# Reordering the parts of a fused attention and feed-forward kernel behind its 292nd part

## The chip, the cores and the metric

The kernel runs on one core of a Trainium2 chip. The metric is device microseconds (us) of one execution, measured on the chip; lower is better. The engines are named as in the profile: PE multiplies matrices, DVE is VectorE, ACT is ScalarE, POOL is GpSimd, and SP issues the transfers (its queue is written SPq). Each engine works through its own instructions in order and waits on semaphores for the others.

## What is computed

```python
# attention: batch 4, heads 8, seq 768, head_dim 64; chunks of 32 keys, the best 6 are kept
k_min, k_max = per chunk minimum and maximum of k
ub   = sum(max(q * k_min, q * k_max))            # an upper bound for each chunk
top  = the 6 chunks with the largest ub, causal by chunk
attn = softmax(scale * q @ k.T, kept chunks and causal only)
x    = (attn @ v) laid out as 3072 tokens x 512
# feed-forward: 512 -> 2048 -> 512
h = x @ w_in
g = h * clip(h + 3, 0, 6) / 6
out = g @ w_out
```

## The kernel before

The 32 heads are 16 pairs i = 0 to 15. From pair 4 on, two pairs form a "quad" n = 2 to 7 (pairs 2n and 2n+1). The 3072 tokens are 8 groups g of 384 tokens, and each group is 3 blocks of 128. A group needs one half of a batch from all 4 pairs of that batch, so groups 2b and 2b+1 come after pairs 4b to 4b+3.

The order of all work is written out by hand: `ORDER` is a string of 1207 parts, and a loop at the end of the kernel calls a small function for each part, in that order. A part is a name and its numbers; letters at its end say which PSUM bank it uses (a, b, c are double banks PBa, PBb, PBc; x, y are single banks PSx, PSy). Each engine receives its instructions in the order of the parts. The parts that matter here:

- `lk.n`, `lq.n` (line 251) load k and q of a quad into a third of STAGE, four transfers each; `kd`, `qd` (line 257, DVE) turn them, `mx`, `mn`, `kx` (DVE) reduce k to chunk bounds, `rp`, `kb`, `qb` (ACT) prepare operands.
- `ud.n` (line 364) is 128 small matmuls for the chunk bounds; `us tr tm se tb tx` (DVE) turn them into a mask, `mv` (line 411, POOL) gathers it, `ms` (line 418) writes it to a scratch tensor SCR in DRAM and `ml.i.u` (line 426) loads pieces of it, replicated, into mask tiles (MX, MY, and free parts of WS and STAGE). Quads 2 and 3 apply the mask by matmuls instead.
- `SQ.n.u` (line 577) makes the scores of both pairs of a quad for one of six units u, into two banks; `ex.i.u` (line 588, ACT) takes the exponential, `af` (line 595, POOL) cuts the diagonal, `mm.i.u` (line 432, DVE) applies the mask.
- `A.i` (12 matmuls) and `B.i.0`, `B.i.1` (15 each) multiply with the values (line 611). A needs units 0 and 1, B needs units 2 to 5. `na`, `nb` (lines 628 and 631, DVE) normalise into XB.
- `xt.g` (line 637) issues three DMA transposes from XB to XT on SP. `H.g.f` (line 655) is 8 matmuls from XT, `hu` (line 663, ACT) and `gt` (line 666, DVE) make the gate GT. `O.g.t.n` (line 691) is 4 of the 16 matmuls of one output block, `ot` (line 698, ACT) copies it out of PSUM and `st` (line 702, SP) stores it.
- The last block, `O.7.2.0`, is made in two column parts (lines 680 to 683: 384 and 128 columns), each with its own ACT copy and store. The parts `O.7.2.1` and on, `ot.7.2` and `st.7.2` do nothing.

A bank is reused when its reader is done: `H` frees its bank after `gt`, `SQ` after `ex`, `A` and `B` after `na` and `nb`, `O` after `ot`, `ud` after `us`.

Of the kernel before, what the change touches and what calls it, by code (L numbers as in the profile page):

```python
# [34 lines left out]
PB LK.0.1.1 PW PI F1.b F0.b PT F4.a PO AQ.0.0.0 PF F3.x F7.c F5.b PZ AK.0.0.1 F6.b PC PR Z.y.6 LK.0.1.0 EG.3  # L35
KT.0.1.b F2.y MN.0.1 AQ.1.0.1 AQ.0.0.1 LK.3.0.1 QT.0.0.x MX.0.1 EG.1 PA RN.0.0 LK.0.0.0 KT.0.0.a MX.0.0 LQ.0.1.0
LQ.0.1.1 QT.0.1.y LK.1.1.0 AQ.1.0.0 LK.2.0.1 LK.1.1.1 MN.0.0 LK.1.0.0 LQ.1.1.0 EG.0 LQ.1.1.1 AK.1.0.1 KB.0.1
QT.1.0.c RN.1.0 RP.0.0 UH.0.0.b UB.0.0 QB.0.0 KT.1.1.x TH.0.0.b MX.1.1 T8.0.0 SE.0.0 KB.0.0 RA.0.1 RP.0.1 UH.0.1.a
UB.0.1 QB.0.1 QB.1.0 LQ.3.0.0 MN.1.1 RP.1.0 QT.1.1.y LH.0.0.b MT.0.0 KT.1.0.c LK.2.0.0 RP.1.1 MX.1.0 MN.1.0 LK.2.1.0
QB.1.1 KB.1.1 LQ.3.0.1 EG.2 S.0.1.b LQ.2.0.1 S.0.0.a ex.0.1 RN.1.1 TH.0.1.x T8.0.1 LQ.2.0.0 LK.3.0.0 KB.1.0 ex.0.0  # L40
af.0.0 UH.1.0.b QT.3.0.y RP.3.0 QB.3.0 SE.0.1 LK.2.1.1 LQ.2.1.1 UB.1.0 UH.1.1.c UB.1.1 KT.2.0.a RN.3.0 QT.2.0.b
RP.2.0 LH.0.1.c MN.2.0 QB.2.0 KT.3.0.y KB.3.0 MT.0.1 LQ.2.1.0 MX.2.0 KT.2.1.x S.0.5.c KB.2.0 RN.2.0 UH.2.0.b
TH.1.0.a ex.0.5 KB.2.1 MX.3.0 S.0.3.c ex.0.3 MN.3.0 af.0.3 T8.1.0 SE.1.0 QT.2.1.y RP.2.1 QB.2.1 UB.2.0 MX.2.1
LH.1.0.b MN.2.1 RA.2.1 TH.2.0.a MT.1.0 T8.2.0 TH.1.1.x UH.3.0.c SE.2.0 T8.1.1 wl.0 bd wc.0 S.1.1.b LK.3.1.1 ex.1.1
af.1.1 LH.2.0.a MT.2.0 UB.3.0 LK.3.1.0 KT.3.1.y KB.3.1 SE.1.1 LV.1.0.1 LQ.3.1.1 S.1.0.a UH.2.1.b MN.3.1 LQ.3.1.0
ex.1.0 UB.2.1 QT.3.1.x RP.3.1 af.1.0 LH.1.1.c MX.3.1 MT.1.1 LV.2.0.1 S.2.1.b S.2.0.a RN.3.1 TH.3.0.y S.0.2.c T8.3.0
af.0.5 ex.2.1 UH.3.1.b SE.3.0 QB.3.1 ex.2.0 LH.3.0.y UB.3.1 TH.2.1.x LV.0.0.1 LV.0.0.0 VC.0.0 MT.3.0 af.2.1 LV.1.0.0
T8.2.1 SE.2.1 S.0.4.b S.1.5.a ex.0.2 ex.1.5 af.2.0 LV.2.0.0 VC.2.0 TH.3.1.y T8.3.1 S.1.3.c ex.0.4 LH.2.1.x af.0.1
MT.2.1 A.2.a na.2 VC.1.0 ex.1.3 A.0.x na.0 lk.2 S.3.0.b ex.3.0 af.3.0 SE.3.1 S.1.2.a ex.1.2 af.1.2 S.3.1.c A.1.y
ex.3.1 LH.3.1.x kd.2.1 af.3.1 na.1 mn.2.1 af.1.5 af.0.2 MT.3.1 S.2.5.b ex.2.5 wl.1 af.2.5 LV.0.1.0 S.1.4.a ex.1.4  # L50
S.2.3.c LV.0.1.1 VC.0.1 X.0.0.x kd.2.0 LV.1.1.1 S.3.3.b mx.2.1 af.1.3 mn.2.0 LV.1.1.0 ex.2.3 S.2.2.a ex.2.2 VC.1.1
B.0.0.y B.0.1.y xe.0.0 LV.3.0.1 S.3.5.c LV.3.0.0 VC.3.0 ex.3.3 S.3.2.a nb.0 lk.3 A.3.x na.3 ex.3.2 LV.2.1.0 B.1.0.b
B.1.1.b nb.1 ex.3.5 af.3.3 X.0.1.y xe.0.1 mx.2.0 kx.2 S.2.4.c ex.2.4 kd.3.0 LV.3.1.1 mn.3.0 S.3.4.b ex.3.4 H.0.1.a
hu.0.1 X.1.0.c kd.3.1 kb.2.0 wc.1 H.0.2.b af.3.5 af.2.2 xe.1.0 af.3.2 LV.2.1.1 VC.2.1 gt.0.1 af.2.3 hu.0.2 B.2.0.y
B.2.1.y nb.2 LV.3.1.0 VC.3.1 B.3.0.x B.3.1.x nb.3 wl.2 gt.0.2 kb.2.1 wc.2 H.0.0.c hu.0.0 gt.0.0 H.0.3.a X.1.1.x
xe.1.1 H.0.5.b hu.0.3 gt.0.3 mx.3.1 hu.0.5 H.1.3.c gt.0.5 hu.1.3 wl.3 H.0.4.a hu.0.4 mn.3.1 H.1.1.b gt.1.3 gt.0.4
hu.1.1 lq.2 qd.2.1 gt.1.1 H.1.2.c hu.1.2 wl.4 wc.3 rp.2.1 wl.5 lq.3 H.0.6.a qd.2.0 gt.1.2 hu.0.6 gt.0.6 mx.3.0
rp.2.0 wc.4 wc.5 H.1.5.b hu.1.5 gt.1.5 qb.2.0 ud.2.a.c us.2.0 us.2.1 kx.3 tr.2.0 H.1.6.b tm.2.0 se.2.0 tb.2.0
O.0.2.0.x O.0.2.1.x hu.1.6 gt.1.6 qd.3.0 mv.2.0 mv.2.1 O.0.0.0.y H.1.4.a qd.3.1 wl.6 lv.4 wc.6 qb.2.1 hu.1.4 rp.3.1
tr.2.1 gt.1.4 tm.2.1 se.2.1 tb.2.1 O.0.0.1.y rp.3.0 H.0.7.b ud.3.a.c mv.2.2 us.3.0 tr.3.0 us.3.1 mv.2.3 kb.3.0  # L60
kb.3.1 O.0.2.2.x hu.0.7 gt.0.7 qb.3.0 H.1.7.a hu.1.7 gt.1.7 SQ.2.3.b.c tr.3.1 O.0.0.2.y tm.3.1 se.3.1 ex.4.3 wl.7
wc.7 SQ.2.2.a.b ex.5.3 O.0.0.3.y tm.3.0 tb.3.1 ex.5.2 af.5.2 lv.5 vc.5 lk.4 ex.4.2 H.1.0.c se.3.0 tb.3.0 mv.3.1 vc.4
ot.0.0 SQ.2.0.b.a hu.1.0 lq.4 gt.1.0 O.0.2.3.x ex.5.0 ot.0.2 O.0.1.0.y ex.4.0 kd.4.1 SQ.2.5.a.c ex.4.5 af.4.5 ex.5.5
af.5.5 af.4.0 qb.3.1 O.0.1.1.y O.0.1.2.y SQ.2.1.c.a mv.3.3 kd.4.0 ex.5.1 mn.4.1 af.5.1 st.0.0 mn.4.0 O.0.1.3.y
SQ.2.4.b.a mx.4.1 ex.4.1 af.4.1 ot.0.1 qd.4.0 O.1.1.0.y O.1.1.1.y af.5.3 af.5.0 qd.4.1 ex.4.4 mx.4.0 kx.4 rp.4.0
rp.4.1 A.5.x na.5 mv.3.0 kb.4.1 ud.4.c.b us.4.0 tr.4.0 us.4.1 tr.4.1 kb.4.0 O.1.1.2.y lv.7 vc.7 mv.3.2 ex.5.4
SQ.3.0.c.a ex.6.0 lv.6 vc.6 ex.7.0 st.0.2 af.6.0 A.4.x na.4 af.7.0 O.1.1.3.y SQ.3.1.b.c ex.7.1 tm.4.0 se.4.0 tb.4.0
ex.6.1 af.7.1 ot.1.1 B.5.0.x lk.5 B.5.1.x SQ.3.5.c.a af.6.1 nb.5 A.7.b na.7 A.6.y O.1.0.0.x na.6 af.4.2 ex.7.5
ex.6.5 af.6.5 qb.4.0 af.4.3 SQ.3.4.a.b tx.4.0 kd.5.0 tm.4.1 mx.5.0 O.1.0.1.x B.4.0.y lq.5 se.4.1 ex.7.4 SQ.3.3.c.b
# [692 lines left out]
```

## Time and profile before

| What | Value |
|---|---|
| Runs of before | 270.97, 271.82, 272.12 us; median 271.82 us |
| Span of the profiled execution | 272.2 us, its own time |
| PE busy | 258.0 us (95%) |
| DVE busy | 210.0 us (77%) |
| ACT busy | 180.5 us (66%) |
| POOL busy | 108.1 us (40%) |
| Transfers of the SP queue | 74.4% of the span of 16 DMA engines |

The profile gives no time for that execution apart from its span, which lies 0.4 us above the median. Busy shares are averages over the whole span; what bounds a stretch has to be read from that stretch.

### The profile page before, as it was taken

To read this page: it belongs to the slowest core of one execution; us is meant where nothing else is said; L and a number is where in the kernel's file an instruction comes from. 1 tells how busy PE (TensorE), PEld (TensorE's weight loads), DVE (VectorE), ACT (ScalarE), POOL (GpSimd) and SP (SyncE) were. 2 spreads that over 40 slices of the span, in tenths; PEclk is the share of its full clock that TensorE was granted. 3 is DMA by queue.
4 is the path that set the end of the run, shared out by engine and by line. 5 is a ranking of instruction groups with operands and counts; after the bars stand their busy time and mean duration, and the time that the engine had idled before them with its cause. 6 is when DMAs were issued, how large, how long until landed. Compare 5 with 4: busy or idle time off the path is not lost.

```text
span 272.2 us, 8580 instructions
## 1 busy us (share of the span) xinstructions
PE 258.0 (95%) x3442; PEld 149.7 (55%) x3442; DVE 210.0 (77%) x506; ACT 180.5 (66%) x249; POOL 108.1 (40%) x243
## 2 busy tenths in 40 slices
...
GB/s 166 203 245 181 257 199 361 250 249 339 197 174 235 135 55 156 303 105 235 209 230 133 206 194 205 179 221 177 124 198 167 213 164 135 45 54 116 39 2 117
DMA packets 105784, 48.80 MB, mean 179 GB/s; under 512 B 87184, under 2 KB 97680, under 8 KB 105744
## 3 DMA queue, kind: packets, MB, share of 16 engines
q1 hardware_dynamic: 103344, 47.66, 74.4%
...
## 4 chain that ended last, share of the span: by engine, by line
PE 63%; DVE 17%; DMA 9%; issue 5%; ACT 3%; SPq 3%; POOL 0%; DVEq 0%; ACTq 0%; POOLq 0%
PE PSy L691 11%; PE PSx L691 8%; PE PBa L655 8%; PE PBc L655 7%; PE PBb L655 5%; DVE GT L666 4%; DMA VS<-in_v_dram 4%; PE PBb L691 3%; PE PSx L611 3%; DVE PT L432 3%; DVE KMA L480 2%; DMA STAGE<-in_q_dram 2%; PE PBa L364 2%; PE PSy L611 2%; PE PBb L577 2%
## 5 line engine op out<-in xcount | busy, mean ns | idle before, releaser
L655 PEld LDWEIGHTS <-WIN 128*128 128x128 bf16 x512 | 49.0, 98 | 37.4 <-issue 4.1
L595 POOL TENSOR_SCALAR_AFFINE_SELECT PT<-PT 128x256 bf16<-128x256 bf16 x78 | 33.0, 443 | 69.2 <-ACT PT L588 68.8
L691 PEld LDWEIGHTS <-GT 128*128 128x128 bf16 x368 | 33.0, 98 | 37.0 <-issue 2.5
L691 PE MATMUL PSy<-WOUT,GT 128*128 128x512 bf16 x176 | 43.8, 380 | 0.0
L691 PE MATMUL PSx<-WOUT,GT 128*128 128x512 bf16 x144 | 35.6, 380 | 0.0
L411 POOL COPY MQA<-MTM 32x144 bf16<-32x144 bf16 x96 | 29.8, 311 | 11.8 <-DVE MTM L397 5.0
L655 PE MATMUL PBc<-XT,WIN 128*128 128x384 bf16 x176 | 32.2, 326 | 1.2 <-DMA XT<-XB 1.1
L655 PE MATMUL PBa<-XT,WIN 128*128 128x384 bf16 x176 | 32.2, 326 | 0.1
L666 DVE SCALAR_TENSOR_TENSOR GT<-U,PBc 128x768 bf16<-128x768 bf16 x22 | 20.9, 950 | 13.4 <-ACT U L663 13.3
L663 ACT ACTIVATE U<-PBc 128x768 bf16<-128x768 f32 x22 | 17.8, 811 | 19.2 <-PE PBc L655 19.1
L588 ACT ACTIVATE PT<-PBa 128x1024 bf16<-128x1024 f32 (+2 forms) x28 | 26.8, 958 | 5.5 <-PE PBb L577 3.5
L655 PE MATMUL PBb<-XT,WIN 128*128 128x384 bf16 x160 | 29.3, 326 | 1.0 <-ACT PT L588 1.0
L666 DVE SCALAR_TENSOR_TENSOR GT<-U,PBa 128x768 bf16<-128x768 bf16 x22 | 20.9, 948 | 11.9 <-ACT U L663 11.7
L663 ACT ACTIVATE U<-PBa 128x768 bf16<-128x768 f32 x22 | 17.9, 812 | 14.4 <-PE PBa L655 11.2
L588 ACT ACTIVATE PT<-PBc 128x1024 bf16<-128x1024 f32 (+2 forms) x26 | 23.6, 906 | 5.0 <-PE PBa L582 1.6
L588 ACT ACTIVATE PT<-PBb 128x1024 bf16<-128x1024 f32 (+2 forms) x24 | 21.5, 895 | 5.0 <-PE PBb L577 2.3
L257 DVE STREAM_TRANSPOSE STAGE<-STAGE 128x768 f32<-128x768 f32 x24 | 22.7, 964 | 1.7 <-DMA STAGE<-in_q_dram 1.5
L611 PEld LDWEIGHTS <-PT 128*128 128x128 bf16 x546 | 19.2, 97 | 6.9 <-issue 2.3
L663 ACT ACTIVATE U<-PBb 128x768 bf16<-128x768 f32 x20 | 16.3, 814 | 9.7 <-PE PBb L655 6.1
L666 DVE SCALAR_TENSOR_TENSOR GT<-U,PBb 128x768 bf16<-128x768 bf16 x20 | 18.9, 946 | 4.2 <-ACT U L663 4.2
L342 DVE TENSOR_REDUCE KMA<-STAGE 128x24 f32<-128x768 f32 x24 | 22.1, 937 | 0.1
L577 PEld LDWEIGHTS <-KBA 32*128 32x128 bf16 x480 | 9.7, 92 | 16.1 <-issue 13.2
...
## 6 DMA issues: line engine op xcount, KB each, us to landing
...
```

Source lines behind the costliest of these rows:

```text
L257: nc.vector.transpose(out=T, in_=T)
L342: nc.vector.tensor_reduce(out=dst, in_=staged("k", n)[:, h], axis=AX.X, op=(A.max, A.min)[w])
L411: nc.gpsimd.tensor_copy(to[:, part], rows)
L432: nc.vector.tensor_tensor(out=T, in0=T, in1=mask_tile(i, u).rearrange("p (k e x) -> p e k x", e=2, x=64), op=A.min)
L577: nc.tensor.matmul(PSB[both[g // 2]][:, g % 2, at:at + w], lhsT=K[rows, x, j * P:(j + 1) * P], rhs=Q[rows, x, q0:q0 + w], start=(x == 0), ...
L588: nc.scalar.activation(pt(i, u)[:, :, 0:n], PSB[slot["S", i, u]][:, :, 0:n], ACT.Exp, scale=float(scale))
L595: nc.gpsimd.affine_select(out=T[:, :, lo:lo + P], in_=T[:, :, lo:lo + P], pattern=[[0, 2], [1, P]], compare_op=A.is_ge, fill=0.0, base=0, ...
L611: nc.tensor.matmul(O[:, e, t, :], lhsT=pt(i, u)[:, e, lo:lo + P], rhs=VB[i % 4][:, j, e, :], start=(j == 0), stop=(j == qb))
L655: nc.tensor.matmul(PSB[c][:, ff, 0:GRP], lhsT=WIN[:, kt, (2 * f + ff) * P:(2 * f + ff + 1) * P], rhs=XT[g % 3][:, kt, :], start=(kt == 0), ...
L663: nc.scalar.activation(slot["R", g, f][:], PSB[slot["H", g, f]][:, :, 0:GRP], ACT.Relu, bias=3.0)
L666: nc.vector.scalar_tensor_tensor(out=GT[g % 2][:, 2 * f:2 * f + 2, :], in0=slot["R", g, f][:], scalar=6.0, in1=PSB[slot["H", g, f]][:, :, ...
L691: nc.tensor.matmul(PSS[c], lhsT=GT[g % 2][:, f, t * P:(t + 1) * P], rhs=WOUT[:, f, :], start=(f == 0), stop=(f == FT - 1))
```

## The change

The first 292 parts stay as they are (the last of them are S.3.4.b and ex.3.4). The other 915 are put into another order, and many are given other banks. No part is added or taken out, and no function changes. The line numbers behind the table are 2 lower afterwards. Two lines of the table as the diff has them, around the transposes of group 6:

```diff
-O.4.1.3.x ot.4.1 B.15.0.b B.15.1.b nb.15 xt.6 H.6.1.c hu.6.1 ml.14.2 mm.14.4 H.6.0.b ml.14.5 af.14.2 mm.14.2 gt.6.1
+ml.15.3 O.5.2.3.x ot.5.2 mm.15.3 B.12.0.c ot.4.1 B.12.1.c ml.14.2 xt.6 af.15.5 mm.15.5 nb.13 af.14.5 H.6.1.a hu.6.1
```

On PE the parts stand at nearly the same depth as before. Counted in PE's own work behind part 292, ud.2, SQ.2.3, H.2.2, SQ.4.0, B.8.0, H.4.0 and the first H.7 do not move at all. Some value products do: A.9 now comes 4.8 us of PE work later, B.10.0 6.1 us, B.12 10.6 us later.

**SP, around the transposes of group 6** (XT <- XB). SCR_110 and SCR_111 are the masks of pairs 14 and 15; OT rows are stores of output. Before:

```order
L702 DMA out_dram<-OT_134 128x512
L426 DMA STAGE<-SCR_111 128x1x768
L426 DMA MX_113<-SCR_110 128x1x768
L426 DMA MX_113<-SCR_110 128x1x256
L426 DMA STAGE<-SCR_111 128x1x768
L426 DMA STAGE<-SCR_111 128x1x256
L702 DMA out_dram<-OT_133 128x512
L426 DMA MY_116<-SCR_111 128x1x768
L426 DMA MY_116<-SCR_111 128x1x256
L637 DMA_TRANSPOSE XT_123<-XB_122 128x4x128 x3
L426 DMA WS_85<-SCR_110 128x1x768
L426 DMA WS_85<-SCR_110 128x1x256
```

Now:

```order
L700 DMA out_dram<-OT_134 128x512
L424 DMA MY_116<-SCR_111 128x1x768
L424 DMA MY_116<-SCR_111 128x1x256
L700 DMA out_dram<-OT_133 128x512
L424 DMA STAGE<-SCR_111 128x1x768
L424 DMA STAGE<-SCR_111 128x1x256
L424 DMA WS_85<-SCR_110 128x1x768
L424 DMA WS_85<-SCR_110 128x1x256
L635 DMA_TRANSPOSE XT_123<-XB_122 128x4x128 x3
L424 DMA STAGE<-SCR_111 128x1x768
L424 DMA STAGE<-SCR_111 128x1x256
L700 DMA out_dram<-OT_132 128x512
```

The load of unit 2 of pair 15 (the second STAGE pair) moved behind the transposes, that of unit 2 of pair 14 (WS_85) in front of them; the load of MX_113 moved further up.

**SP, around the load of q for quad 6.** SCR_104 and SCR_105 are the masks of pairs 8 and 9, XT_123 the transposes of group 3. Before:

```order
L637 DMA_TRANSPOSE XT_123<-XB_122 128x4x128 x3
L426 DMA WS_85<-SCR_104 128x1x768
L426 DMA WS_85<-SCR_104 128x1x256
L426 DMA MY_115<-SCR_105 128x1x384
L426 DMA MY_115<-SCR_105 128x1x256
L426 DMA MX_114<-SCR_104 128x1x768
L251 DMA STAGE<-in_k_dram 32x24x64 x4
L702 DMA out_dram<-OT_134 128x512
L426 DMA MX_112<-SCR_104 128x1x384
L426 DMA MX_112<-SCR_104 128x1x256
L251 DMA STAGE<-in_q_dram 32x24x64 x4
```

Now:

```order
L635 DMA_TRANSPOSE XT_123<-XB_122 128x4x128 x3
L416 DMA SCR_104<-MQA 128x1x1152
L260 DMA VS_69<-in_v_dram 128x12x64
L424 DMA MY_116<-SCR_105 128x1x768
L424 DMA MY_116<-SCR_105 128x1x256
L424 DMA MX_114<-SCR_104 128x1x768
L249 DMA STAGE<-in_q_dram 32x24x64 x4
```

Between the transposes and the load of q there were seven mask pieces, a store and the load of k; now there are three mask pieces, a load of v and the mask write SCR_104, which stood three rows above the transposes before.

**SP, the end of the program.** Before:

```order
L702 DMA out_dram<-OT_134 128x512
L702 DMA out_dram<-OT_132 128x512
L702 DMA out_dram<-OT_133 128x512
L683 DMA out_dram<-OT_134 128x384
L683 DMA out_dram<-OT_134 128x128
```

Now:

```order
L681 DMA out_dram<-OT_134 128x384
L681 DMA out_dram<-OT_134 128x128
L700 DMA out_dram<-OT_132 128x512
L700 DMA out_dram<-OT_133 128x512
L700 DMA out_dram<-OT_134 128x512
```

The block that is stored in two parts is no longer the last one; the program ends with a whole block of 512 columns.

## Rows read from the trace of the kernel before

**Rows 1.** The page, part 1: busy us, share of the span, instructions.

```profile
PE 258.0 (95%) x3442; PEld 149.7 (55%) x3442; DVE 210.0 (77%) x506; ACT 180.5 (66%) x249; POOL 108.1 (40%) x243
```

**Rows 2.** Stretches: us, then PE, PEld, DVE, ACT, POOL busy, clock, DMA, GB/s.

```profile
50.00:60.00 10.00, 8.80 (x115) 5.38 (x115) 10.00 (x13) 7.43 (x10) 4.02 (x3) 1.00 1.05 288
140.00:150.00 10.00, 9.11 (x126) 5.29 (x126) 9.93 (x17) 8.29 (x13) 7.82 (x13) 1.00 0.48 151
232.00:260.00 28.00, 28.00 (x167) 15.04 (x164) 12.02 (x14) 11.02 (x16) 0.00 (x0) 1.00 0.23 61
```

**Rows 3.** Waits of PE: line waited for; us in total, times, longest.

```profile
PE PBa L364 <- DVE GT L666: 1.2, 1, 1.2
PE PBc L655 <- DMA XT<-XB: 1.1, 1, 1.1
PE PBb L655 <- ACT PT L588: 1.0, 1, 1.0
PE PBc L577 <- issue: 0.9, 1, 0.9
```

**Rows 4.** The chain that ended last, late stretch: start us, us, what.

```profile
231.55 0.91 PE PSx L611 x30
240.25 1.30 PE PBa L655 x8
241.55 0.86 PE PSy L691 x4
```

**Rows 5.** Timelines of PE, DVE and SP, 157 to 168 us.

```profile
157.09 0.61 PE L611 MATMUL PBc<-VB,WS 128*128 128x65 bf16 x12
158.03 0.56 DVE L631 TENSOR_TENSOR XB<-PBc,RINV 128x384 bf16<-128x384 f32 x1
159.04 0.52 SPq L426 DMA_DIRECT2D MX<-SCR  x1
159.66 4.81 SPq L637 DMA_TRANSPOSE XT<-XB  x3
167.04 1.46 PE L655 MATMUL PBb<-XT,WIN 128*128 128x384 bf16 x8 [1.03 <-ACT PT L588]
```

**Rows 6.** Timelines of PE, DVE and SP, 215 to 227 us.

```profile
215.14 0.53 PE L611 MATMUL PSx<-VB,WS 128*128 128x65 bf16 x12
215.94 0.56 DVE L631 TENSOR_TENSOR XB<-PSx,RINV 128x384 bf16<-128x384 f32 x1
215.72 1.24 SPq L426 DMA_DIRECT2D STAGE<-SCR  x2
217.64 1.18 SPq L426 DMA_DIRECT2D MY<-SCR  x2
218.91 3.84 SPq L637 DMA_TRANSPOSE XT<-XB  x3
226.19 1.46 PE L655 MATMUL PBc<-XT,WIN 128*128 128x384 bf16 x8 [1.14 <-DMA XT<-XB]
```

**Rows 7.** Timelines of SP, DVE and PE, 127 to 149 us.

```profile
127.06 2.48 SPq L251 DMA_DIRECT2D STAGE<-in_q_dram  x4
135.32 1.84 DVE L257 STREAM_TRANSPOSE STAGE<-STAGE 128x768 f32<-128x768 f32 x2 [1.54 <-DMA STAGE<-in_q_dram]
142.69 1.09 PE L611 MATMUL PSx<-VB,PT 128*128 128x65 bf16 x30 [0.29 <-DVE PT L432]
148.48 0.47 PE L611 MATMUL PSx<-VB,PT 128*128 128x65 bf16 x10 [0.60 <-DVE RINV L628]
```

**Rows 8.** ACT at the end; landing of stores at L683, then at L702.

```profile
265.37 0.60 ACT L698 ACTIVATE OT<-PBb 128x512 f32<-128x512 f32 x1 [0.27 <-PE PBb L691]
268.86 0.28 ACT L682 ACTIVATE OT<-PBa 128x128 f32<-128x128 f32 x1 [0.40 <-PE PBa L680]
DMA to landing us min/median/max: 1.9/1.9/2.0
DMA to landing us min/median/max: 2.0/2.9/5.3
```

More of the change, by code (lines that the diff above doesn't have):

```diff
@@ L34 @@
 ORDER = """
[L35 to L69, printed above, removed]
```

123 lines of the change are left out of this document (78 added, 45 removed).

## Prediction

> **What bounds the kernel now.** I read four views in this order: the busy shares, the stretches, the waits of PE, and the timelines around each long wait. The busy shares show PE at 258.0 of 272.2 us [rows 1]; the reader should see from them that this change has little room. Nothing in it takes work from PE, and the 14.2 us in which PE is idle include the start, the end and the part before the 292nd, which stays. Late in the run PE is full: 28.00 of 28 us from 232 to 260 [rows 2]. There each `H` costs 1.30 us, a quarter of an `O` 0.86 us and a pair of `B` 0.91 us, start to start [rows 4]. So the new order can only win back time in which PE stood still.
>
> The waits of PE name where that is, behind part 292 [rows 3]. One wait of 1.2 us for a gate (line 666) before `ud.2`; 1.1 us for the transposes before `H.6.1`; 1.0 us before `H.4.0`; 0.9 us with no releaser that the profile shows, in `SQ.2.3`. Two shorter ones, 0.29 and 0.60 us, stand at `B.8` and `A.9` [rows 7]. Together that is 5.1 us, 1.9% of the span, and the most that this reading can give back.
>
> The wait of 1.0 us before `H.4.0` is put down to an ACT instruction. I read it as a wait for the transposes, by two rows [rows 5, 6]: in both places the first `H` starts 7.3 to 7.4 us after the first transpose was issued (159.66 to 167.04, and 218.91 to 226.19). That is the time that a group needs from its first transpose to its first matmul.
>
> **The change part by part.** The amount of work is the same on every engine, so each term is a wait that goes or comes.
>
> *Transposes of group 6.* `A.15` ends at 215.7, its normalise at 215.94 + 0.56 = 216.5, but SP was still issuing mask loads and a store and reached the transposes at 218.91 [rows 6]: 2.4 us lost in SP's queue. In the new order mask loads are earlier in front of them or behind them; of what stands directly in front, the load of unit 2 of pair 14 needs only `mm.13.2`, which DVE has before `na.15`. PE now has less work between `A.15` and `H.6.1`: seven `O` quarters, two `B` pairs and one `SQ` instead of eight, two and one, so 0.9 us less. The chain needs about 0.8 us to the normalise's end plus 7.3 us, 8.1 us; PE has 7 x 0.86 + 2 x 0.91 + 0.55 = 8.4 us. The wait of 1.14 us should go: -1.0 us (bounds 0 and -1.14).
>
> *Transposes of group 4.* The normalise of `A.11` ended at 158.03 + 0.56 = 158.6 and the transposes went out at 159.66, behind a mask load at 159.04 [rows 5]. That load now stands earlier. But DVE gets a k reduction of 0.94 us in front of `na.10` and `na.11`, which may eat part of the 1.1 us: -0.7 us (bounds 0 and -1.03).
>
> *DVE behind the load of q for quad 6.* The load was issued from 127.06 on and DVE stood still for 1.54 us until 135.32, waiting for its last piece [rows 7]. Right after, DVE is busy 9.93 of 10 us from 140 to 150 [rows 2], so this delay goes through to `B.8` and `A.9`. The new SP order issues that load earlier, DVE has `mm.8.2` after fewer long instructions, and `A.9` stands 4.8 us of PE work later. Both waits should go: -0.9 us (bounds 0 and -0.9).
>
> *The gate before `ud.2`.* From 50 to 60 us DVE is busy 10.00 of 10 [rows 2], and `ud.2` waits for `gt.0.6` behind it. In the new order the same number of instructions stands in front of `gt.0.6`; only one copy of about 0.5 us moves in front of a gate that DVE has to wait for anyway. `H.1.5` takes the bank of `H.1.2` instead of `H.1.1`, so a part of the wait moves one place forward. I take -0.4 us (bounds 0 and -1.2).
>
> *The gap in `SQ.2.3`.* The row shows no releaser [rows 3], so nothing says that another order removes it. The parts in front of it are the same set, in another sequence. I leave it at 0 (bounds 0 and -0.9).
>
> The Trainium skill (Runtime: NRT & Kernel Launch, Instruction fetch mechanics) says that an engine's instructions are fetched in blocks of 256 through a DMA queue of their own, ahead of use. By that rule a gap from a late fetch would stay where the instruction count puts it, and the sum would be the same; no row here shows that it is one.
>
> *The end.* Before, the last ACT copy takes 0.28 us and its store lands in 2.0 us. Now the last copy is one of 512 columns, 0.60 us, and a whole block's store lands in 2.0 us at best [rows 8]. +0.3 us for the copy and 0.1 us for the larger store: +0.4 us (bounds 0.3 and 1.2, the median landing of 2.9 us).
>
> The Trainium skill (DMA: Bandwidth & Descriptors, Anatomy of one DMA) gives, for transfers issued by GpSimd, 2.0 us plus the bytes at 436 GB/s. By it a store of 256 KB instead of 64 KB would cost 0.45 us more, an estimate from that page, and the sum would be 0.4 us worse; the landing rows of late stores are closer together than that.
>
> *New waits.* Two hand-overs of banks got shorter: `SQ.3.0` takes a bank of `ud.4` after one `A` instead of one `O`, and `H.5.7` follows its bank's last user by one `H` and one `O`. A reordering of 915 parts makes more of these than I can follow. I take +0.4 us (bounds 0 and 1.5).
>
> Sum: -1.0 - 0.7 - 0.9 - 0.4 + 0.4 + 0.4 = **-2.2 us**. Made against the profiled execution it gives 272.2 - 2.2 = 270.0 us; that execution is 0.4 us above the median of the runs, 271.8, so for a median I say **269.6 us**.
>
> **The rivals.** A difference under 0.5%, 1.4 us, cannot be told from no change here.
>
> *The waits only move.* PE is at 95%, DVE at 99% in one stretch. Where DVE is the bound behind PE, an earlier load lets it start earlier but it still has the same 9.9 us of work, and PE meets it a few parts later. Then I keep only the two transpose waits, 1.7 us, and pay the end and new waits at 1.5: 271.8 - 1.7 + 0.4 + 1.0 = 271.5 us. For it: PE does the same work at the same depth. Against it: the two transpose waits come from SP's queue, and DVE's load of 210 us is an average with room on both sides of that stretch.
>
> *Slower: the transposes of groups 6 and 7 become too tight.* This is one mechanism at one place, the last 55 us. PE work between `A.15` and `H.6.1` falls from 9.3 to 8.4 us, and between `B.14` and the first `H.7` from 11.2 (four `H`, seven `O`) to 9.1 us (three and six), while the chain stays at 8.1 us with nothing ahead of it. It decides when SP reaches the transposes more than 0.3 us late for group 6 or 1.0 us late for group 7; from there each us costs PE one. If SP is as late as before, 2.4 us [rows 6], group 6 waits 2.1 us (1.0 more than before) and group 7 waits 1.4 us. With the end and the new waits at 1.5, and the middle giving 0.7 back: 271.8 + 1.0 + 1.4 + 0.4 + 1.5 - 0.7 = 275.4 us; half of that lateness gives about 273.5. For it: seventeen mask loads and four stores of 0.6 us each must go out between the last mask write and the first of these transposes. Against it: the masks of quad 7 get ready earlier, since its `ud` moved 0.9 us forward.
>
> *The gap in `SQ.2.3` goes as well*, and all bounds on the good side hold: 271.8 - 1.14 - 1.03 - 0.9 - 1.2 - 0.9 + 0.3 = 266.9 us.
>
> **How the numbers follow.** My forecast, a gain of 1.4 to 3.9 us, gets 0.56; the full gain 0.05; waits that only move 0.29; too tight 0.10. Range: the forecast's own bounds go from 267.9 to 270.4. To hold 8 in 10 it must take in the waits that only move, so up to 272.1, and a part of the full gain, so down to 267.4. Faster by over 0.5% (under 270.4): 0.61. Within 0.5%: 0.29. Slower: 0.10.
>
> **What would show it.** In the new profile the waits of PE should no longer have a line of 1 us for the transposes or before `H.4.0`; from the normalise of `A.15` to the first transpose should be under 0.5 us. DVE should have no wait for a load of q. `ud.2` should still wait, about 0.8 us. The end should have one ACT copy of 0.60 us. I am wrong if PE's waits sum to as much as before under other names, if a DVE stretch near 140 is full and PE waits at its `A` and `B` again, or if the first `H.6` and `H.7` wait over 1 us for XT.

## The result and the profile after

| | before | changed |
|---|---|---|
| Median | 271.68 us (4 runs, 270.97 to 272.12) | 274.99 us (4 runs, 273.73 to 275.51) |
| Ratio | | 1.0138, interval 1.0092 to 1.0184 |
| Span of the profiled execution | 272.2 us | 273.8 us |

The changed order is slower; I had forecast 269.6 us, a gain. Twelve more runs of the changed kernel beside 29 of the one before (e5 below) give a smaller loss, 1.25 us between the medians and a ratio of 1.0069 with an interval from 1.0031 to 1.0107: the first four drew a large one. The ratios leave out runs over 1.5% above the fastest of the same kernel, a varying share of the runs here; so medians of all runs stand beside them below.

The busy shares of the changed kernel, against [rows 1]:

```profile
PE 259.8 (95%) x3442; PEld 150.5 (55%) x3442; DVE 210.8 (77%) x506; ACT 180.0 (66%) x249; POOL 107.7 (39%) x243
```

The same work on every engine, as it must be. The same stretches as [rows 2] (us, then busy of PE, PEld, DVE, ACT, POOL, clock, DMA, GB/s), and one that was unremarkable before:

```profile
50.00:60.00 10.00, 8.98 (x56) 5.28 (x54) 9.45 (x12) 6.50 (x9) 3.45 (x3) 1.00 1.13 305
140.00:150.00 10.00, 10.00 (x121) 5.64 (x118) 8.48 (x14) 9.38 (x14) 7.36 (x16) 1.00 0.79 184
156.00:164.00 8.00, 6.26 (x163) 3.88 (x162) 5.11 (x18) 1.02 (x2) 0.00 (x0) 0.79 0.28 76
232.00:260.00 28.00, 28.00 (x183) 15.67 (x181) 14.80 (x18) 11.29 (x15) 0.00 (x0) 1.00 0.18 52
```

From 140 to 150 us PE is now full (9.11 of 10 before), as forecast. From 156 to 164 us it loses 1.7 us and runs on a lower clock; before it was full there. The waits of PE, against [rows 3]:

```profile
PE PSx L609 <- DVE WS L430: 1.7, 1, 1.7
PE PSx L642 <- DVE MTM L540: 1.6, 1, 1.6
PE PBc L653 <- DVE GT L664: 1.0, 1, 1.0
PE PSy L609 <- DVE XT L646: 0.9, 1, 0.9
```

None of the four long waits of before stands where it was. Four others stand in their place, in this order at `A.11`, `X.0.0`, `H.1.5` and `B.2.0`; the one at `H.1.5` is the old wait for a gate ahead of `ud.2`, one place further forward. The second (`X.0.0`, at 34.58 us) lies ahead of part 292, and SP's first load from behind part 292 goes out only at 36 us or later, so the change can't have made it. Before it was 0.4 us.

Where the loss of that trace is: PE, DVE and SP around `A.11` and `ud.6`, against [rows 5].

```profile
156.71 0.22 PE L609 MATMUL PSx<-VB,WS 128*128 128x65 bf16 x2
158.66 0.48 PE L609 MATMUL PSx<-VB,WS 128*128 128x65 bf16 x10 [1.74 <-DVE WS L430]
151.78 0.35 DVE L430 TENSOR_TENSOR PT<-PT,WS 128x384 bf16<-128x384 bf16 x1
158.25 0.36 DVE L430 TENSOR_TENSOR WS<-WS 128x384 bf16<-128x384 bf16 x1 [2.92 <-DMA WS<-SCR]
152.05 0.54 SPq L700 DMA_DIRECT2D out_dram<-OT  x1
152.68 0.52 SPq L424 DMA_DIRECT2D WS<-SCR  x1
153.31 0.52 SPq L700 DMA_DIRECT2D out_dram<-OT  x1
160.88 4.44 SPq L635 DMA_TRANSPOSE XT<-XB  x3
```

The masks of unit 1 of all pairs share one tile, so `mm.10.1` (151.78) must be done before the load `ml.11.1` (152.68) may start, and `mm.11.1` (158.25) waits for it: landed at 158.16, 5.5 us after its issue. Before, the same load went out at 152.75 and landed after 3.8 us. Two stores of 256 KB stand right around it now. `H.4.0` itself has no wait any more; the stall has moved ahead of it.

The transposes of group 6, against [rows 6]:

```profile
217.84 0.20 DVE L626 RECIPROCAL RINV<-PBa 128x6 f32<-128x6 f32 x1 [0.44 <-PE PBa L609]
218.07 0.56 DVE L629 TENSOR_TENSOR XB<-PBa,RINV 128x384 bf16<-128x384 f32 x1
218.66 3.84 SPq L635 DMA_TRANSPOSE XT<-XB  x3
226.10 1.46 PE L653 MATMUL PBa<-XT,WIN 128*128 128x384 bf16 x8
```

From the end of the normalise (218.63) to the first transpose is 0.03 us, against 2.4 us, and the wait of 1.14 us is gone. DVE no longer waits for a load of q near 135 us and `B.8` starts without a wait, against [rows 7]:

```profile
138.96 0.96 DVE L255 STREAM_TRANSPOSE STAGE<-STAGE 128x768 f32<-128x768 f32 x1
142.89 0.63 PE L609 MATMUL PSx<-VB,PT 128*128 128x65 bf16 x15
```

The end, against [rows 8]:

```profile
267.97 0.60 ACT L696 ACTIVATE OT<-PSy 128x512 f32<-128x512 f32 x1 [1.99 <-PE PSy L689]
269.75 0.60 ACT L696 ACTIVATE OT<-PBa 128x512 f32<-128x512 f32 x1 [1.18 <-PE PBa L689]
```

One copy of 0.60 us, and its store lands at 272.38 us, 2.0 us after its issue, as forecast.

### The profile page after: what moved, and what is told of

Read it like the earlier page. It is cut to its first block, busy times and chain, and to the rows that moved or that the text cites. A ratio compares the mean times of both kernels' runs of the same rounds, so it can differ in the third digit from the quotient of the medians.

```text
span 273.8 us, 8570 instructions
## 1 busy us (share of the span) xinstructions
PE 259.8 (95%) x3442; PEld 150.5 (55%) x3442; DVE 210.8 (77%) x506; ACT 180.0 (66%) x249; POOL 107.7 (39%) x243
## 4 chain that ended last, share of the span: by engine, by line
PE 71%; DVE 13%; DMA 7%; POOL 3%; ACT 2%; issue 2%; DVEq 0%; ACTq 0%; POOLq 0%
PE PSx L689 11%; PE PSy L689 11%; PE PBc L653 8%; PE PBa L653 7%; PE PBb L653 7%; DMA WS<-SCR 3%; DVE PT L430 3%; DVE GT L664 3%; PE PBa L689 3%; PE PBc L575 2%; PE PSy L609 2%; DVE KMA L478 2%; DMA VS<-in_v_dram 2%; PE PBa L362 2%; PE PSx L609 2%
## 5 line engine op out<-in xcount | busy, mean ns | idle before, releaser
L593 POOL TENSOR_SCALAR_AFFINE_SELECT PT<-PT 128x256 bf16<-128x256 bf16 x78 | 31.7, 430 | 62.8 <-ACT PT L586 62.0
L689 PE MATMUL PSy<-WOUT,GT 128*128 128x512 bf16 x160 | 40.7, 385 | 0.0
L689 PE MATMUL PSx<-WOUT,GT 128*128 128x512 bf16 x160 | 39.7, 380 | 0.0
L409 POOL COPY MQA<-MTM 32x144 bf16<-32x144 bf16 x96 | 31.1, 324 | 17.7 <-DVE MTM L395 8.7
L653 PE MATMUL PBc<-XT,WIN 128*128 128x384 bf16 x184 | 33.7, 326 | 1.3 <-DVE GT L664 1.0
L653 PE MATMUL PBa<-XT,WIN 128*128 128x384 bf16 x168 | 30.7, 326 | 0.0
L586 ACT ACTIVATE PT<-PBa 128x1024 bf16<-128x1024 f32 (+2 forms) x27 | 25.4, 941 | 7.6 <-PE PBa L575 4.4
L586 ACT ACTIVATE PT<-PBc 128x1024 bf16<-128x1024 f32 (+2 forms) x27 | 25.0, 927 | 2.8 <-PE PBa L580 1.4
L664 DVE SCALAR_TENSOR_TENSOR GT<-U,PBa 128x768 bf16<-128x768 bf16 x21 | 19.9, 949 | 8.0 <-ACT U L661 8.0
L664 DVE SCALAR_TENSOR_TENSOR GT<-U,PBc 128x768 bf16<-128x768 bf16 x23 | 21.8, 946 | 4.1 <-ACT U L661 4.0
```

The lines of the kernel that those rows point to most:

```text
L409: nc.gpsimd.tensor_copy(to[:, part], rows)
L586: nc.scalar.activation(pt(i, u)[:, :, 0:n], PSB[slot["S", i, u]][:, :, 0:n], ACT.Exp, scale=float(scale))
L593: nc.gpsimd.affine_select(out=T[:, :, lo:lo + P], in_=T[:, :, lo:lo + P], pattern=[[0, 2], [1, P]], compare_op=A.is_ge, fill=0.0, base=0, ...
L653: nc.tensor.matmul(PSB[c][:, ff, 0:GRP], lhsT=WIN[:, kt, (2 * f + ff) * P:(2 * f + ff + 1) * P], rhs=XT[g % 3][:, kt, :], start=(kt == 0), ...
L664: nc.vector.scalar_tensor_tensor(out=GT[g % 2][:, 2 * f:2 * f + 2, :], in0=slot["R", g, f][:], scalar=6.0, in1=PSB[slot["H", g, f]][:, :, ...
L689: nc.tensor.matmul(PSS[c], lhsT=GT[g % 2][:, f, t * P:(t + 1) * P], rhs=WOUT[:, f, :], start=(f == 0), stop=(f == FT - 1))
```

## The experiments

All moves below are of whole parts; nothing else differs. "Order of before from part 700 on" means: the first 700 parts of one order, and after them those still missing, in the sequence of the other. Each group of runs (e1 to e4, e5 to e8, e9 to e12, e13 to e16, e17 and e18) shares one chip and its own runs of the kernel before. Each kernel has twelve runs, e7 six.

| Run | Edit | Median of all | Of before | Difference | Ratio (interval) |
|---|---|---|---|---|---|
| e1 | before again | 272.32 | 272.41 | -0.1 | 1.0009 (0.9972 to 1.0046) |
| e2 | new, mask chain mended | 273.69 | 272.41 | +1.3 | 1.0052 (1.0014 to 1.0090) |
| e3 | new to part 700 only | 272.59 | 272.41 | +0.2 | 1.0051 (1.0012 to 1.0090) |
| e4 | new from part 700 only | 275.04 | 272.41 | +2.6 | 1.0062 (1.0014 to 1.0110) |
| e5 | new again | 274.28 | 273.03 | +1.25 | 1.0069 (1.0031 to 1.0107) |
| e6 | new, `ud.6` later | 274.68 | 273.03 | +1.65 | 1.0079 (1.0037 to 1.0120) |
| e7 | new from 700 to 890 only | 275.81 | 273.03 | +2.8 | 1.0118 (1.0068 to 1.0168) |
| e8 | new from 890 only | 273.70 | 273.03 | +0.7 | 1.0042 (1.0006 to 1.0078) |
| e9 | new to 890 only | 273.29 | 273.26 | 0.0 | 1.0037 (0.9997 to 1.0077) |
| e10 | new, masks behind `na.13` | 274.34 | 273.26 | +1.1 | 1.0027 (0.9983 to 1.0070) |
| e11 | e2 + e10 + old end | 272.42 | 273.26 | -0.8 | 0.9993 (0.9953 to 1.0032) |
| e12 | e2, old from 890 | 274.25 | 273.26 | +1.0 | 0.9999 (0.9951 to 1.0048) |
| e13 | new, old end | 272.82 | 272.54 | +0.3 | 1.0016 (0.9982 to 1.0050) |
| e14 | new, stores early | 274.10 | 272.54 | +1.6 | 1.0056 (1.0027 to 1.0085) |
| e15 | e11 + stores early | 272.83 | 272.54 | +0.3 | 1.0015 (0.9975 to 1.0055) |
| e16 | before, stores late | 273.55 | 272.54 | +1.0 | 1.0069 (1.0031 to 1.0106) |
| e17 | before, `xt.6` earlier | 271.97 | 271.57 | +0.4 | 1.0014 (0.9977 to 1.0052) |
| e18 | e17 + `lq.6` earlier | 270.85 | 271.57 | -0.7 | 0.9948 (0.9909 to 0.9986) |

Twelve runs of one kernel spread over 2.5 to 9 us, and two medians of a dozen runs can differ by about 1 us by that alone. Medians and ratios do not always agree either: e3, e8 and e9 lie 0.2, 0.7 and 0.0 us over the kernel before by the medians, and 0.5, 0.4 and 0.4% (1.4, 1.1 and 1.0 us) by the ratios. So beside the times I read every trace by stretches: each part of PE gets its median duration from the first trace of before, and for each trace I note when PE has done the same amount of work. The change of that lag over a stretch is what the stretch cost more or less than in the first trace of before:

| Stretch there (us) | e1 | new | e5 | e2 | e9 | e14 | e15 | e17 | e18 |
|---|---|---|---|---|---|---|---|---|---|
| to 39 (unchanged parts) | +1.64 | +0.93 | +1.78 | +0.72 | +1.10 | -0.09 | -0.23 | +0.72 | +1.15 |
| 39 to 72 (`B.2`, gates, `ud.2`) | -0.94 | +0.67 | +0.68 | +0.67 | +1.69 | +0.67 | +0.67 | -0.93 | -0.93 |
| 72 to 78 (`SQ.2.3`) | -0.60 | -0.93 | -0.30 | -0.84 | -0.11 | -0.58 | -0.84 | -0.72 | 0.00 |
| 139 to 150 (q load, `B.8`, `A.9`) | -0.66 | -0.97 | -0.80 | -0.97 | -0.97 | -0.80 | -0.80 | +0.44 | -0.67 |
| 150 to 160 (`A.11`) | +0.06 | +3.30 | +1.40 | -0.18 | -0.03 | +1.50 | +0.36 | +0.37 | -0.07 |
| 160 to 172 (`H.4.0`) | -1.09 | -1.09 | -1.09 | -1.09 | -1.09 | -1.09 | -1.10 | -0.04 | -0.48 |
| 203 to 223 (`A.13`) | 0.00 | +0.49 | +0.88 | +0.84 | 0.00 | +1.21 | -0.47 | 0.00 | 0.00 |
| 223 to 234 (`H.6.1`) | +0.38 | -1.29 | -1.30 | -1.29 | -1.30 | -1.30 | -1.20 | -1.02 | -1.30 |
| end | +0.04 | +0.77 | +0.77 | +0.78 | -0.45 | +0.37 | -0.01 | -0.05 | -0.49 |

**The base.**

> The kernel before, once more, for the base of the sum. If the time of a run lies 1.7 us above its span, as in all runs of the changed kernel, the profiled execution with its span of 272.15 us was one of about 273.9 us, and a new one of about 271.7 us has a span of about 270.0 us; the parts that came 1.3 us earlier in the changed kernel's unchanged prefix show how much of that is jitter ahead of part 292. If the base was right, the span is 271.5 to 272.2 us again and the 1.7 us belong to the changed kernel alone. Time 271.0 to 272.2 us either way.

Span 271.0 us, time 272.73 us: 1.7 us apart, as in every run here that has both, to 0.1 us. By that the first trace of before, span 272.15 us, belongs to an execution of 273.9 us, outside the three runs shown. The second trace has other waits of PE:

```profile
PE PSx L644 <- DVE MTM L542: 2.2, 1, 2.2
PE PBc L655 <- DMA XT<-XB: 1.5, 1, 1.5
PE PBa L364 <- DVE GT L666: 1.2, 1, 1.2
PE PBc L577 <- issue: 0.3, 1, 0.3
```

The wait of 1.0 us before `H.4.0` is not there at all, that in `SQ.2.3` is 0.3 instead of 0.9 us, and DVE waits 0.78 us for the load of q, not 1.54. Three of the five waits that I meant to win are partly an accident of one execution.

**Cutting the order in two, at parts 700 and 890.**

```diff
-parts 292 to 1206: the order of before
+parts 292 to 699: the new order
+the parts left over: the order of before
```

(e3; e4 is the reverse; e8 and e9 the same with 890; e7 has the new order from 700 to 890.)

> Parts 292 to 700 in the new order, the rest as before. 'Mask chain': the loss lies behind part 700, so the time is that of before, 271.0 to 272.2, or up to 1 us less, since the wait for the load of q for quad 6 goes. 'Spread': about half of the loss, 273.0 to 273.8. 'Head': all of it, 274.5 or more.

> Parts 292 to 700 as before, the rest in the new order. 'Mask chain': all of the loss, 274.3 to 275.5, with a wait of over 1 us in A.11 for mm.11.1 in the trace. 'Spread': about half, 273.0 to 273.8. 'Head': as before, 271.0 to 272.2.

> Parts 700 to 890 in the new order (A.8 to H.4, some 137 to 180 us), all others as before. 'Mask chain': the whole loss of the kernel whose tail alone was new, so a median of 274.3 to 275.5 over all runs, half of them with a clock of 0.994 or less. 'Late' (the loss comes behind part 890, from the waits at 200 to 215 us and the end): 271.7 to 272.9.

> Parts 890 to the end in the new order, all before them as before. 'Mask chain': nothing of the loss, and the transposes of group 6 go out earlier, so 270.8 to 272.4. 'Late': 274.0 to 275.5. My forecast of +0.4 us for the end and -1.0 us for the transposes of group 6 would put it at 271.8 against 272.4 for the kernel before in that job.

> Parts 292 to 890 in the new order, the rest as before. In two jobs the changed order lay 1.3 us over the kernel before (medians of all runs), its head alone (to part 700) 0.2 us and its late part alone 0.7 us. 'Late' (new waits of about 1 us at A.13, where na.12 stands behind masks, and 0.35 us at the end): +0.2 to +0.7 us over the kernel before in this job, and no wait at A.13. 'Middle' (the wait in A.11 and what follows, parts 700 to 890): +1.0 to +1.6 us, with a wait for mm.11.1 in A.11 in the trace.

By the medians the head alone costs 0.2 us, the late part alone 0.7, head and middle together nothing; by the ratios they cost 0.5, 0.4 and 0.4%, with intervals that overlap. So the times rank no part above another. They do speak against "mask chain", which put all of the loss in the middle: the head and the late part, each without the new middle, have intervals above 1. e4 and e7, which were to show the middle, don't: where the old head meets the new middle, `SQ.5.0` waits for a gate, in e7

```profile
PE PBb L575 <- DVE GT L664: 3.1, 2, 2.9
```

a wait that neither whole order has. A cut is evidence only if its seam is clean in the trace.

**The mask chain and the two stores.**

```diff
 mm.9.3
+mm.10.1 ml.11.1
 ml.10.3
...
 na.8 st.2.0
-mm.10.1
 O.3.0.0.x
...
 hu.3.4
-ml.11.1
 vc.11
```

> The changed order, with mm.10.1 moved behind mm.9.3 on VectorE and the load ml.11.1 ahead of ml.10.3 on SP. Theory 'mask chain' (the loss is the late last link of the chain of masks of unit 1, which ends before A.11, and what follows from it): ml.11.1 goes out near 150.2 instead of 152.7, lands before 156, the wait of 1.7 us in A.11 goes, and the time falls by 1.2 to 2.5 us, to 272.5 to 273.8. Theory 'spread' (many small waits, each worth 0.2 to 0.5 us): the wait goes, but the time stays within 0.7 us of 275.0. Theory 'head' (lost ahead of part 700 and carried on): no change, 274.5 to 275.4.

> The changed kernel once more, for its spread over a dozen runs and a second trace. 'Mask chain': the chain of unit 1 ends so close to A.11 that the length of one load decides; so the runs spread, some near 272 us without the wait in A.11, most near 275; median of all runs 274.3 to 275.5, and the trace of a run under 273 has no wait over 0.5 us in A.11, that of a run over 274.5 has one. 'Spread': the traces of all runs have the same row of small waits, and the runs lie within 2 us of each other.

e2's trace has no wait in `A.11`, yet the median falls to +1.3 us only, and e5, with the order as it was, is at +1.25 us. e5's wait is shorter than in the first trace (its load landed after 5.0 us):

```profile
159.66 0.48 PE L609 MATMUL PSx<-VB,WS 128*128 128x65 bf16 x10 [1.25 <-DVE WS L430]
```

In the traces with the chain as the new order has it, `ml.11.1` takes 5.5, 5.0, 5.0, 4.2, 4.1, 3.5, 3.1 and 2.5 us (new, e5, e7, e10, e6, e4, e9, e13), and `A.11` waits 1.7, 1.3, 1.0, 0.5, 0.5, 0.2, 0 and 0 us: the longer this one load, the longer the wait. The old middle has the same load; it takes 3.6 to 4.3 us in seven traces, and the wait is 0 to 0.6 us. e12's trace shows what else stands in the way; its time says little, +1.0 us by the medians and no difference by the ratio.

```diff
 parts 292 to 889: as in the run with the mask chain mended
-parts 890 to 1206: the new order
+the parts left over: the order of before
```

> The changed order up to part 890 with the chain of masks of unit 1 mended, the rest as before. 'Middle': 0.5 us or more under the kernel with the late part old alone, so -0.3 to +0.4 us against the kernel before. 'Late': within 0.4 us of the kernel with the late part old alone. 'Head': both kernels stay at +0.7 us or more, since the mended chain gives nothing back to a head that is late.

```profile
160.18 0.60 ACT L696 ACTIVATE OT<-PSx 128x512 f32<-128x512 f32 x1 [2.01 <-DMA out_dram<-OT]
160.83 0.54 PE L609 MATMUL PSx<-VB,WS 128*128 128x65 bf16 x12 [1.31 <-ACT OT L696]
```

The mask is in time, but now the copy `ot.3.0` waits for `st.2.0`, issued at 155.13 and landed 4.9 us later, since the ring has three output buffers; `A.11` waits for the copy, since it takes its bank. e11 shows the same (1.97 and 1.27 us). At this place two transfers must be in time, and either was late in some trace. So I moved the stores:

```diff
 ml.10.1
+st.2.0 st.2.1
 SQ.5.4.c.b
...
 na.8
-st.2.0
 mm.10.1
...
 B.9.0.c
-st.2.1
 gt.3.4
```

> The changed order with the two stores st.2.0 and st.2.1 moved ahead in SP's queue, behind ml.10.1 (about 148 us instead of 152 and 153 us), nothing else. 'Stores' (at A.11 either ml.11.1 comes late beside the two stores, or the copy ot.3.0 waits for st.2.0 to land, by how long the transfers of that moment take): no wait over 0.6 us in A.11 by either way, median 0.4 to 1.0 us lower than the changed order, +0.3 to +0.9 us over the kernel before. 'Mask chain' (the load is late for its own reasons): the wait in A.11 stays, +1.0 to +1.6 us.

```profile
157.61 0.48 PE L609 MATMUL PSx<-VB,WS 128*128 128x65 bf16 x10 [1.36 <-DVE WS L430]
```

The stores now go out at 147.31 and 147.89 us, and the load still takes 4.7 us and `A.11` still waits: in this trace the load is late without the stores beside it. The opposite trial, stores late in the order of before:

```diff
-st.2.0
 mm.9.3
...
-st.2.1
 O.3.0.0.x
...
 O.3.2.1.y
+st.2.0
 ml.11.1
+st.2.1
 mm.11.1
```

> The kernel before, with st.2.0 moved directly ahead of ml.11.1 and st.2.1 directly behind it, as the new order has them; nothing else. 'Stores': +0.4 to +1.5 us over the kernel before, with a wait of A.11 for mm.11.1 or for ot.3.0 in the trace. 'Mask chain': ml.11.1 goes out 0.6 us later at most and nothing follows, -0.3 to +0.5 us.

+1.0 us, but not by the mechanism: its trace has no wait for `mm.11.1` or `ot.3.0`, and the mean granted clock was under 0.996 in ten of its twelve runs (in two to six of twelve in the others). In the traced one it was half from 21.2 to 28.1 us, ahead of everything that the edit moves. It says nothing for the stores; why the clock fell so often here, no run shows.

**`ud.6` right behind `A.11`.**

```diff
 na.11 ex.11.5 mm.10.3
-ud.6.a.c us.6.1 us.6.0 tr.6.0 tm.6.0
 O.3.2.1.y O.3.2.2.y
+ud.6.a.c us.6.1 us.6.0 tr.6.0 tm.6.0
 O.3.1.0.x
```

> The changed order, with ud.6 and the VectorE steps on it moved behind O.3.2.2, so that the small matmuls of ud.6 do not follow A.11's directly, as before. 'Mask chain': the wait in A.11 is as long as before the edit, so the median stays within 0.6 us of the changed kernel's in the same job. 'Clock' (the loss is the clock's fall to half in ud.6 and behind it): runs with a mean clock of 0.994 or less become rarer than one in five and the median falls by 0.8 to 1.7 us.

+1.65 us, no better; "clock" falls as a steady cause. In the first trace of the new order the clock did fall here: the stretch costs 3.3 us, 1.7 of them the wait, and the rest is about half of the 3.4 us that ran at half the clock (more below). But e5 has a wait of 1.25 us and the same sequence at full clock.

**`A.13`, and the end.**

```diff
 A.12.x ml.15.5
-mm.13.5
 SQ.7.5.b.c
-mm.13.3
 na.12
...
 na.13
+mm.13.5 mm.13.3
```

> The changed order with the masks mm.13.5 and mm.13.3 moved behind na.13 on VectorE, nothing else. B.13 alone needs them, 10 us of PE work later. 'Late': the waits of A.13 and SQ.7.4 (0.3 to 1.2 us together) go, and the median falls to +0.2 to +0.7 us over the kernel before. 'Middle': the waits go and the median stays at +1.0 to +1.6 us. A third way: the two masks turn up late at B.13 or hold up a load behind them, +1.3 us or more.

In e5 `A.13` waits for the normalise of `A.12`, which stands behind masks that no `A` needs; in e10 that wait is gone:

```profile
210.05 0.52 PE L609 MATMUL PSx<-VB,PT 128*128 128x65 bf16 x12 [0.82 <-DVE XB L629]
```

```profile
208.25 0.53 PE L609 MATMUL PSx<-VB,PT 128*128 128x65 bf16 x12
```

By the stretches it gives back 0.6 us (203 to 223 us: +0.78 on average over eight traces, +0.21 in e10), the median hardly moves (+1.1 against +1.25 us). The end alone:

```diff
 parts 292 to 1119: the new order
-parts 1120 to 1206: the new order
+the parts left over: the order of before
```

> The changed order with the parts from 1120 on as before (the last blocks' output, copies and stores), nothing else. 'End': 0.35 us for the last copy and its store, and whatever the new tail costs beside: +0.6 to +1.0 us over the kernel before in this job, where the changed order lay at +1.3 us. 'Waits' (the loss is the waits in the middle and at A.13): +1.0 to +1.6 us.

+0.3 us against +1.25: more was won than either theory said, and "end" (+0.6 to +1.0) is the nearer. Its trace shows 0.1 us less than the first trace of before behind the last matmul; the new end has 0.77 us more there, the same to 0.01 us in five of eight traces.

**All mended.** e11 has the chain, the masks and the old end; e15 the early stores too.

```diff
+mm.10.1, ml.11.1, mm.13.5, mm.13.3 as above; from part 1120 on the order of before
+e15 only: st.2.0 st.2.1 behind ml.10.1
```

> The changed order with three costs undone: the chain of masks of unit 1 (mm.10.1 behind mm.9.3, ml.11.1 ahead of ml.10.3), the masks of pair 13 behind na.13, and the end from part 1120 on as before. If the loss is the sum of these places, up to 0.5 us for the chain, 0.9 us for A.13, 0.35 us for the end, the gains that I forecast stand free: -0.7 to 0.0 us against the kernel before in this job. If the loss sits elsewhere (the head, which keeps a late start that the old order absorbs; SP's last drain, 0.45 us), +0.4 us or more.

> Stores early, chain of unit 1 mended, masks of pair 13 behind na.13, end as before, all else in the new order. If these four places are the loss, it is at or under the kernel without the first of them, which lay 0.8 us under the kernel before with an interval from -2.0 to +0.35 us: -1.5 to -0.5 us. If the rest of the new order costs as much as it wins, -0.3 to +0.5 us.

-0.8 and +0.3 us: level with before, and 1 to 2 us better against it than the whole new order (0.5 to 0.8% by the ratios). With these places mended the loss is gone, and nothing of the forecast gain shows either. e11's own trace still waits in `A.11`, so it is the two kernels together, more than one trace, that this rests on. e15's trace is the shortest of all, 268.6 us, with no wait in `A.11`, at `A.13`, at `H.4.0` or `H.6.1`. What it keeps is the head:

```profile
PE PBc L653 <- DVE GT L664: 1.0, 1, 1.0
PE PSy L609 <- DVE XT L646: 0.9, 1, 0.9
```

**The forecast gains alone, in the order of before.**

```diff
 mm.13.3
-ml.14.4
 B.13.0.b
...
 nb.15 xt.6
+ml.14.4
 H.6.1.c
```

> The kernel before, with one mask load of SP, ml.14.4, moved from ahead of the transposes of group 6 to behind them; nothing else. It makes the first of my terms alone: from na.15 to the first transpose under 1 us instead of 2.4, no wait of PE over 0.3 us for XT at the first H.6. If the term is what I forecast (-1.0 us, up to -1.5 by the second trace of the kernel before): -0.8 to -1.5 us. If another wait of that place takes over (B.15, B.14, the masks behind the transposes): -0.3 to +0.5 us.

```diff
 gt.3.3
+lq.6
 lk.7
...
 ex.8.3
-lq.6
 qd.6.0
```

> As the last one, and the load of q for quad 6 moved ahead of that of k for quad 7 on SP. It adds the term of VectorE behind that load (-0.9 us as forecast, -0.3 by the second trace of the kernel before). Both terms real: -1.5 to -2.4 us against the kernel before, no wait of VectorE for STAGE near 135 us. Absorbed (VectorE meets the same stretch of full work, or k of quad 7 is late instead): within 0.4 us of the run with the transposes alone.

In e17 SP reaches the transposes at 217.21 instead of 218.91 us and `H.6.1` has no wait, 1.0 us in the stretch; the median doesn't show it. In e18 they go out at 216.26 us and DVE has no wait for q:

```profile
216.26 3.85 SPq L635 DMA_TRANSPOSE XT<-XB  x3
133.96 1.83 DVE L255 STREAM_TRANSPOSE STAGE<-STAGE 128x768 f32<-128x768 f32 x2
```

By the ratio the two moves together are faster than before, 0.9948 with an interval from 0.9909 to 0.9986: the best of all kernels here. Being the best of many, and 0.7 us by the medians, it would need a second group of runs to be sure. The ratio makes it 1.4 us; both terms together were 1.9 us.

## Why the prediction was wrong

It said -2.2 us. Set against that, per stretch, the mean of all traces that have the old or the new order there (traces whose edit or seam lies in the stretch left out):

| Term | Stretch | Old order (traces) | New order (traces) | New less old | Forecast |
|---|---|---|---|---|---|
| Gate before `ud.2`, and `B.2.0` | 39 to 72 | -0.66 (8) | +0.92 (12) | +1.6 | -0.4, and in +0.4 |
| Gap in `SQ.2.3` | 72 to 78 | -0.46 (8) | -0.71 (12) | -0.25 | 0 |
| Load of q, quad 6 | 139 to 150 | -0.08 (5) | -0.88 (12) | -0.8 | -0.9 |
| `A.11` (a new wait) | 150 to 160 | +0.25 (6) | +1.03 (5) | +0.8 | in +0.4 |
| Transposes of group 4 | 160 to 172 | -0.58 (7) | -1.09 (10) | -0.5 | -0.7 |
| `A.13` (a new wait) | 203 to 223 | 0.00 (9) | +0.78 (8) | +0.8 | in +0.4 |
| Transposes of group 6 | 223 to 234 | -0.70 (7) | -1.25 (11) | -0.55 | -1.0 |
| End | behind the last matmul | -0.10 (12) | +0.62 (8) | +0.7 | +0.4 |

Together +1.8 us, between the 1.25 us of a dozen runs and the 3.3 us of the first four. About 1.6 us of the +3.30 of the first new trace at `A.11` come from the clock's fall there; without them that row is +0.5 and the sum 1.5 us.

- **New waits, +0.4 (bounds 0 to 1.5): the step that failed most.** Three places alone, `B.2.0`, `A.11` and `A.13`, cost about 0.8 us each, 2.4 us together, and none was among those that I named (`SQ.3.0`, `H.5.7`, which show no wait). For `A.11` and `A.13` the order on DVE shows it, and e2 and e10 take it away: a mask ahead of a normalise that PE needs first, and a mask that lets a load of 2.5 to 5.5 us start, some 4 us ahead of its user.
- **`B.2.0`.** What I did not see is the bank of `X.1.0`, y instead of c. `B.2.0` takes y three parts later and waits 0.9 us until DVE has copied it out, in all traces of the new head but one. Before, then changed:

```profile
43.81 1.20 PE L611 MATMUL PSy<-VB,PT 128*128 128x65 bf16 x27 [0.68 <-POOL VB L460]
```

```profile
45.30 1.07 PE L609 MATMUL PSy<-VB,PT 128*128 128x65 bf16 x30 [0.93 <-DVE XT L646]
```

The wait of before, for POOL's cast of v, stands in that trace alone. In e1, e8, e16, e17 and e18, which start 0.5 to 2.9 us late, the cast comes at most 0.6 us later and the wait is 0 to 0.1 us; in e4 and e7 the cast comes 2 us earlier. So a late start is partly made up there. The new wait is 0.92 to 0.93 us however late the start.

The bank alone does not make the new wait. Ahead of the copy DVE has `kx.2` (line 345). In the eleven traces that wait it takes 1.3 us and ends just after POOL's cast of weights `wc.1`; in the eight of the old head it takes 0.2 to 0.4 us. The new order puts four cuts (`af`) ahead of `wc.1` on POOL, which starts at 40.95 us instead of 37.58. In the twelfth trace, e10, with the same order and bank, the cast is over before `kx.2` starts, and `B.2.0` waits 0.16 us. Changed, then e10:

```profile
40.95 1.89 POOL L269 CAST WIN<-WS 128x2048 bf16<-128x2048 f32 x1
41.59 1.31 DVE L345 TENSOR_TENSOR KMA<-KMA 128x48 f32<-128x48 f32 x1
```

```profile
41.14 1.89 POOL L269 CAST WIN<-WS 128x2048 bf16<-128x2048 f32 x1
43.15 0.21 DVE L345 TENSOR_TENSOR KMA<-KMA 128x48 f32<-128x48 f32 x1
45.81 1.07 PE L609 MATMUL PSy<-VB,PT 128*128 128x65 bf16 x30 [0.16 <-DVE XT L646]
```

So the wait needs the bank and the slow `kx.2` together. This is read from the traces; a run with the bank or the cast put back was not made. The same meeting of `kx.3` (0.8 to 1.6 us) with a cast of weights stands in e6, e9, e10 and e12, and only there PE has another wait for a gate, of 0.6 to 1.4 us, between 62 and 66 us.

- **Gate before `ud.2`.** I read 1.2 us of waiting there and took 0.4 of it as won. It is 1.1 to 1.2 us in every trace of the old head, and in the new one 1.0 us in every trace, one place further forward, at `H.1.5`, which takes the bank of `H.1.2`. The move is as I had it; it gives 0.2 us.
- **Transposes of group 4.** Right in kind: SP reaches them 0.03 us after the normalise in every trace of the new middle (0.4 to 1.1 us in the old one), and `H.4.0` has no wait over 0.1 us. The size was one trace's: in the old order that wait is 1.0, 0.8, 0.6 or 0 us.
- **Transposes of group 6: half of the cause was missed.** I put the wait down to SP's being 2.4 us late, and nothing else. In e9, which has the late part of before, SP is 2.5 us late as well, in e10, with the new order, 2.2 us, and `H.6.1` waits in neither. What goes with the wait is the landing of the third transpose: 4.5 to 4.6 us after its issue in the three traces that wait over 1 us (the first, e1 and e7), 2.5 us in all others that show it. The third transpose of group 6 in the first trace of before, then in e9:

```profile
DMA to landing us min/median/max: 4.6/4.6/4.6
DMA to landing us min/median/max: 2.5/2.5/2.5
```

With 2.5 us in the first trace XT would have been complete at 224.0 us, about 1 us before PE came to it; issued 2.4 us earlier, even the slow one would have landed by 223.7 us (both are estimates from these rows). So the wait took a late issue and a slow landing together. The 7.3 us from the first transpose to the first matmul, on which I built this term and the slower rival, were not what a group needs: they held a transpose of 4.6 us in both places that I read. In each of the three traces a transfer of 16 KB on the instruction queue q8 starts 2.0 us after that transpose's issue; in no other does one start less than 2.3 us after it. That it holds the transpose up was not tested. The wait is gone in all eleven traces of the new late part, as forecast; but it stands in only three of seven of the old one (1.1, 1.5 and 1.1 us), 0.5 us on average, which is what the stretch gives.
- **Load of q.** Right in kind and size, 0.8 us of 0.9.
- **End.** The copy and the store were right, 0.35 us of 0.4. The other 0.4 us are SP's, below. By the Trainium skill (DMA: Bandwidth & Descriptors, Anatomy of one DMA) the store four times as large would have taken 0.45 us longer, an estimate with the figures given there for transfers issued by GpSimd; the two traces have 1.97 and 2.01 us.
- **Base.** I took the span of the profiled execution for its time and so set the median 0.4 us under it; by the 1.7 us between span and time the median is 2.1 us under that execution. That alone takes 1.7 us off what the execution could teach about the median: it was one with more waits than usual.
- **The slower rival** (group 6 and 7 too tight) did not happen. "The waits only move" was nearest, and it had 0.29; it counted on waits of the same size, not on larger ones. (Its sum adds 0.4 and 1.0 us where its text says 1.5.) Of my own signs of being wrong, the first came true, PE's waits under other names: those of over 0.1 us with a releaser sum, behind part 292, to 4.5 and 5.1 us in the two traces of the changed order and to 5.1 and 3.4 us in the two of before.
